# Queries, keys and values laid out queue by queue in a retention and mixture-of-experts kernel

## The chip, the cores and the metric

The kernel runs on one core of one Trainium2 chip. The metric is the device time of one execution in microseconds (us). Before the change it is 428.4 us, the median of three runs (426.91, 428.40, 432.99).

## The reference

A retention layer (attention with a decay in the place of the softmax) over 8 batches, 8 heads, 576 positions and 64 values per head, then a layer of 8 experts on the 4608 tokens of width 512 that come out. The core of it:

```python
scores = scale * np.matmul(q, k.transpose(0, 1, 3, 2))
Dmat = np.where(rel >= 0, gamma[:, None, None] ** rel[None, :, :], 0.0)
attn = np.matmul(scores * Dmat[None, :, :, :], v)

x = attn.transpose(0, 2, 1, 3).reshape(B * S, H * D)
do_compute = x @ w_skip > 0          # other tokens stay as they are
xc = x[do_compute]
e_idx = np.argmax(xc @ w_gate, axis=1)
for e in range(E):
    mask = e_idx == e
    y[mask] = gate_w[mask, None] * (np.maximum(xc[mask] @ w1[e], 0.0) @ w2[e])
out[do_compute] = xc + y
```

## The kernel before

The retention runs chunk by chunk. A group g (36 of them, `NT`) is 128 tokens: one chunk of 64 positions of two batches, all 8 heads. Nine groups in a row (`NQ`) make up the sequence of one pair of batches. Each group has a tile `u` of 128 partitions and 4 x 512 values of 4 bytes, so 8 KB per partition and 1 MB in all: the first half (s = 0 and 1) holds queries and keys for the scores, the second half (s = 2 and 3) holds values and keys by rows for the running state. Five such tiles exist (`UBUFS`).

The loop over g does one step per group. TensorE (PE) interleaves the state product of g (L528) with the scores of g + 1 (L476), then multiplies the values of g - 1 (L556), transposes the finished group g - 2 (L578), and now and then works on the router's logits (L586) and on ranks (L233). VectorE (DVE) multiplies the scores by the decay and puts them back into `u` (L494), and takes the products out (L567). GpSimd (POOL) scales the keys of g + 2 by a decay into `kn` (L514), which reads the second half of that group's `u`; two `kn` buffers exist. ScalarE (ACT) copies the state into the next group's `u` (L539), takes the transposed rows out (L580) and issues their store to `out` (L581).

All loads of `u` are issued on SyncE (SP), one for each half, at L436 in `load_half`: 72 of them, 512 KB each. Four groups are loaded ahead of the loop (`UAHEAD`). In step g, the second half of group g + 3 is issued behind the first block of products (a dependency written by hand on the last product so far), and the first half of group g + 4 behind the products of the values of g - 1, which free the buffer. So a half is issued some two and a half to three and a half steps before TensorE needs it. The order on TensorE is the program's own (a manual schedule); other engines keep the order that the tile framework gives them.

In the array that the host prepares, `qkv`, the 512 KB of one load lie in one piece: 128 rows, one per partition, of 1024 values (4096 bytes), group after group and half after half.

From 137.5 us on SP also loads the first expert's weights (L130, 512 KB each, register-addressed), with 64 such loads over the whole program. The experts follow, one after another: two matrix products (L387) with weights and activations each split into a high and a low part (L139, L140), gathers of tokens from `out` (L303) and scatters of results to it (L836).

Of the kernel before, what the change touches and what calls it, by code (L numbers as in the profile page):

```python
# [22 lines left out]
NTOK, DM, NE, DF = B * S, H * D, 8, 1024  # L23
P = 128
NT = NTOK // P
# [2 lines left out]
NCC = DM // P  # L28
NFC = DF // P
NBLK = 3  # L30

CAPS = (368, 344, 332, 308, 304, 286, 278, 276)
CAP = CAPS[0]
# [23 lines left out]
def kernel(  # L57
# [36 lines left out]
    make_identity(nc, ident)  # L94
    iota = const.tile([P, NBLK * P], F16, tag="iota", name="iota")
    nc.gpsimd.iota(iota, pattern=[[1, NBLK * P]], base=0, channel_multiplier=0, allow_small_or_imprecise_dtypes=True)
    desc = const.tile([P, NE], F32, tag="desc", name="desc")
# [79 lines left out]
    def route_b(ps, first, late, pin, n, t0, ex, mb, cb):  # L177
        c0 = NE * NCMP * NBLK + t0 * NE
        pr = ps[:, c0 : c0 + n * NE]
# [44 lines left out]

    def slot_match(t, nb=NBLK):

        r = rs_t[t] = rt.tile([P, NBLK * P], BF16, tag="r", name=f"r_{t}", bufs=NR)
        nc.vector.tensor_scalar(r[:, : nb * P], iota[:, : nb * P], trank[:, t : t + 1], None, ALU.is_equal)  # L228

    def slot_add(ps, t, first, last, nb=NBLK):  # L230
        r = rs_t.pop(t)
        for k in range(nb):
            nc.tensor.matmul(  # L233
                ps[:, k * NE * NCMP : (k + 1) * NE * NCMP],
                r[:, k * P : (k + 1) * P],
                mc[:, t, :],
                start=first and k == 0,
                stop=last,
                skip_group_check=True,
            )  # L240
# [174 lines left out]
    with ExitStack() as actx:  # L415
# [17 lines left out]
        def load_half(g, s, after=None):  # L433
            if s == 0:
                u_t[g] = ap.tile([P, 4, 2, NPR, D], F32, tag="u", name=f"u_{g}", bufs=UBUFS)
            half = nc.sync.dma_start(  # L436
                u_t[g][:, s : s + 2].rearrange("p s c a i -> p (s c a i)"),
                qkv[g, s // 2],
            )
            if after is not None:  # L440
                tc.add_manual_dep(
                    half.ins,
                    after.name,
                    mybir.DependencyInfo(mybir.DependencyClass.Sync, mybir.DependencyReason.DATA),
                    reason="the second half begins behind a block of products",
                )

        def load_u(g):
            for s in (0, 2):
                load_half(g, s)  # L450
# [241 lines left out]
        for g in range(NT):  # L692
            ahead = g + 1 < NT
            for c in range(2):
                in_turn(state(g, c), *([scores(g + 1, c)] if ahead else []))
                if c == 0 and g and g + UAHEAD - 1 < NT:
                    load_half(g + UAHEAD - 1, 2, last_product())
# [8 lines left out]
            if g + UAHEAD < NT:  # L706
                load_half(g + UAHEAD, 0)
# [15 lines left out]
        g = NT  # L723
# [332 lines left out]
```

## Time and profile before

| | |
|---|---|
| median of three runs | 428.4 us |
| the profiled execution | 428.38 us |
| its span, first to last instruction | 426.6 us |
| mean granted TensorE clock | 0.971 |
| HBM read, written | 77.98 MB, 14.55 MB |
| loads of `u` from `qkv` | 72, of 512 KB each |
| first and last issue of them | 0.8 and 146.5 us |
| loads of weights | 64, of 512 KB each |
| stores of `out` by the retention | 36, of 256 KB each |

The profile's engines are PE (TensorE's matmul; PEld its weight load, which runs beside it), DVE, ACT, POOL and SP; a name with a q behind it (SPq, PEq) is the engine's sequencer, where DMAs are issued and waits are held. A name like L436 is a line of the kernel. A row such as "psc<-u" names the tile written and the tile read. The busy strips cut the span into 40 slices of 10.7 us with the busy share in tenths. "DMA share" is the mean busy share of the core's 16 DMA engines. The queue q1 carries what SP issues, q10 what ACT issues, q0 what POOL issues; q8 and q14 bring instructions. Landing is the time from a DMA's issue to its completion.

### The profile page before, as it was taken

The numbers are of one execution on the slowest core, as the hardware profiler recorded it, in microseconds if no ns is written. First come the engines' busy times: TensorE is split into PE (matmuls) and PEld (weight loads), VectorE is DVE, ScalarE is ACT, GpSimd is POOL, SyncE is SP. The second block draws the span as 40 slices with busy tenths as digits, with TensorE's granted clock in tenths as the row PEclk, the third lists the DMA queues.
The fourth block names the chain that finished last, engine by engine and source line by source line (L and its number), as shares of the span: only waits on it lengthen the run. The fifth ranks groups of instructions, "written<-read, shape, count | busy, mean of one in ns | idle before, by whom it ended". The sixth has DMA issues, their size and how long they took to land.

```text
span 426.6 us, 13158 instructions
## 1 busy us (share of the span) xinstructions
PE 383.3 (90%) x5482; PEld 349.2 (82%) x5484; DVE 272.9 (64%) x570; ACT 176.1 (41%) x296; POOL 148.9 (35%) x166
## 2 busy tenths in 40 slices
PE   7888777978796878999999999999999999999990
PEld 3676666866675756888999999999999999999980
DVE  2567694688579888948745565775665665656430
ACT  1334343354344446216444434444534445455210
POOL 5833643364365468060150043032042151400302
PEclk9989998999999889999999999999999999999996
DMA  8889997999989985363765456456456466652101
GB/s 305 310 290 339 311 325 249 328 334 305 311 296 349 338 315 163 103 220 117 267 201 181 148 171 211 149 189 205 163 177 221 154 222 204 199 157 89 52 2 53
DMA packets 29135, 93.05 MB, mean 218 GB/s; under 512 B 3960, under 2 KB 4344, under 8 KB 29072
## 3 DMA queue, kind: packets, MB, share of 16 engines
q1 hardware_dynamic: 19584, 71.31, 50.2%
q0 software_dynamic: 3728, 11.04, 7.6%
q10 hardware_dynamic: 5760, 9.82, 6.1%
q8 instruction: 44, 0.72, 0.7%
q14 instruction: 19, 0.16, 0.1%
HBM read 77.98 MB, written 14.55 MB: 217 GB/s over the span
## 4 chain that ended last, share of the span: by engine, by line
PE 44%; DMA 22%; issue 16%; DVE 10%; POOL 4%; ACT 1%; another core or an unknown queue 1%; POOLq 0%; ACTq 0%; SPq 0%
DMA out<-rs,sidx 15%; PE py L387 10%; PE ph L387 9%; PE pxt L556 7%; PE ps_s L528 5%; PE px L578 4%; DMA xg<-out,gidx 3%; PE psc L476 3%; DVE u L494 2%; POOL out L836 2%; DVE r L228 2%; PE pl L586 2%; DMA out<-xn 1%; DMA u<-qkv 1%; POOL xg L303 1%
## 5 line engine op out<-in xcount | busy, mean ns | idle before, releaser
L140 DVE TENSOR_TENSOR wlo_w<-w,whi_w 128x1024 fp32r<-128x1024 f32 x59 | 71.9, 1223 | 56.5 <-ACT whi_w L139 56.4
L514 POOL TENSOR_TENSOR kn<-u,tt_sb 64x512 f32<-64x512 f32 x64 | 67.5, 1054 | 74.3 <-DMA u<-qkv 51.5
L836 POOL DMA_INDIRECT out<-rs,sidx x24 | 32.7, 1363 | 151.0 <-DVE rs L835 147.7
L139 ACT CAST whi_w<-w 128x1024 fp32r<-128x1024 f32 x59 | 61.6, 1051 | 57.5 <-PE py L387 53.9
L387 PE MATMUL py<-hhi,whi_w 128*128 128x344 f32 (+6 forms) x224 | 70.2, 313 | 0.0
L494 DVE TENSOR_TENSOR u<-psc,dt_sb 64x512 f32<-64x512 f32 x72 | 49.6, 689 | 30.9 <-PE psc L476 15.7
L387 PE MATMUL ph<-xhi,whi_w 128*128 128x344 f32 (+6 forms) x224 | 68.9, 307 | 0.0
L387 PE MATMUL py<-hhi,wlo_w 128*128 128x344 f32 (+6 forms) x224 | 67.7, 302 | 0.0
L387 PE MATMUL ph<-xhi,wlo_w 128*128 128x344 f32 (+6 forms) x224 | 67.7, 302 | 0.0
L387 PE MATMUL ph<-xlo,whi_w 128*128 128x344 f32 (+6 forms) x224 | 67.7, 302 | 0.0
L387 PE MATMUL py<-hlo,whi_w 128*128 128x344 f32 (+6 forms) x224 | 67.5, 302 | 0.0
L539 ACT COPY u<-ps_s 64x512 f32<-64x512 f32 x64 | 37.1, 579 | 46.7 <-PE psc L476 18.3
L528 PEld LDWEIGHTS ps_s<-u,kn 64*64 64x64 f32 x1024 | 36.9, 142 | 21.5 <-issue 13.1
L476 PE MATMUL psc<-u 64*64 64x64 f32 x1152 | 47.8, 230 | 7.0 <-issue 6.9
L556 PE MATMUL pxt<-u 128*64 128x64 f32 x1152 | 46.0, 233 | 8.3 <-issue 8.3
L395 ACT ACTIVATE hhi<-ph 128x344 fp32r<-128x344 f32 (+8 forms) x61 | 26.0, 426 | 64.3 <-PE ph L387 62.1
L528 PE MATMUL ps_s<-u,kn 64*64 64x64 f32 x1024 | 43.2, 231 | 9.9 <-issue 8.4
L556 PEld LDWEIGHTS pxt<-u 128*64 128x64 f32 x1152 | 39.9, 145 | 13.6 <-issue 11.3
L476 PEld LDWEIGHTS psc<-u 64*64 64x64 f32 x1152 | 41.0, 141 | 8.1 <-issue 7.7
L387 PEld LDWEIGHTS ph<-xhi,whi_w 128*128 128x128 f32 x224 | 42.3, 189 | 0.1
L387 PEld LDWEIGHTS ph<-xlo,whi_w 128*128 128x128 f32 x224 | 42.3, 189 | 0.1
L387 PEld LDWEIGHTS py<-hlo,whi_w 128*128 128x128 f32 x224 | 42.3, 189 | 0.0
(178 smaller groups left out, 641.3 us busy)
## 6 DMA issues: line engine op xcount, KB each, us to landing
u<-qkv SPq DMA_DIRECT2D x72, 512.0 KB, 5.8
w<-w SPq DMA_DIRECT2D x64, 512.0 KB, 3.6
out<-xn ACTq DMA_DIRECT2D x36, 256.0 KB, 5.9
out<-rs,sidx POOLq DMA_INDIRECT x24
xg<-out,gidx POOLq DMA_INDIRECT x21
dt_sb<-dtab ACTq DMA_DIRECT2D x1, 128.0 KB
gt_sb<-dtab ACTq DMA_DIRECT2D x1, 128.0 KB
wg_sb<-wg ACTq DMA_DIRECT2D x1, 64.0 KB, 8.3
```

Source lines behind the costliest of these rows:

```text
L139: nc.scalar.copy(hi, t)
L140: nc.vector.tensor_tensor(lo, t, hi.bitcast(F32), ALU.subtract)
L387: nc.tensor.matmul(ps, x, y, start=first and n == 0, stop=last and n == 3 * len(terms) - 1)
L395: nc.scalar.activation(hi, ph, AF.Relu)
L476: nc.tensor.matmul(psc_t[g][halves[j], c, a, :], u[halves[j], 1 - j, c, a, :], u[halves[j], j, c, a, :], start=c == 0 and a == 0, stop=c = ...
L494: nc.vector.tensor_tensor(u_t[g][h, j], psc[halves[j]], tab, ALU.mult)
L514: nc.gpsimd.tensor_tensor(kn_t[g][h], u_t[g][h, 2 + j], tab, ALU.mult)
L528: nc.tensor.matmul(ps_s[halves[j], c, a, :], kn_t[g][h, c, a, :], u_t[g][h, 3 - j, c, a, :], start=n == 0 and c == 0 and a == 0, stop=c == ...
L539: nc.scalar.copy(u_t[g + 1][halves[j], 3 - j], ps_s[halves[j]])
L556: nc.tensor.matmul(pxt[halves[j], a, c * D : (c + 1) * D], u_t[g][:, 3 - j, c, a, :], u_t[g][:, j, c, a, :], start=c == 0 and a == 0, stop ...
L578: nc.tensor.transpose(px[:, c * P : (c + 1) * P], xt_t[b][:, c, o * P : (o + 1) * P], ident)
L836: put = nc.gpsimd.indirect_dma_start(out=out, out_offset=bass.IndirectOffsetOnAxis(ap=sidx[:n, k, e : e + 1], axis=0), in_=rs[:n], in_offs ...
```

## The change

The host puts `qkv` into another order. Its 128 rows per load are seen as 16 times 8, and the 16 becomes the outermost dimension of the whole array: first all of piece 0 (8 rows of group 0's first half, 8 rows of its second half, 8 rows of group 1's first half, and so on), then all of piece 1. A piece has 36 x 2 x 8 rows of 4096 bytes, which is 2.36 MB. The load takes the same 128 rows into the same 128 partitions: its source is now 16 runs of 32 KB at a distance of 2.36 MB instead of one run of 512 KB. In the access pattern of the DMA that is a dimension of 16, one of 8 and one of 1024 values on the side of the source, against 128 partitions and 1024 values on the side of the tile; before, both sides had 128 and 1024.

No instruction is added, removed or moved on any of the engines, and no wait is changed.

```diff
+NQUEUE = 16
...
 def load_half(g, s, after=None):
     if s == 0:
         u_t[g] = ap.tile([P, 4, 2, NPR, D], F32, tag="u", name=f"u_{g}", bufs=UBUFS)
     half = nc.sync.dma_start(
         u_t[g][:, s : s + 2].rearrange("p s c a i -> p (s c a i)"),
-        qkv[g, s // 2],
+        qkv[:, g, s // 2],
     )
...
+    def by_queue(x):
+
+        x = x.reshape(*x.shape[:2], NQUEUE, P // NQUEUE, x.shape[-1])
+        return np.ascontiguousarray(x.transpose(2, 0, 1, 3, 4))
+
...
-    qkv = qkv.reshape(NT, 2, P, 2 * DM)
+    qkv = by_queue(qkv.reshape(NT, 2, P, 2 * DM))
```

## The prediction

> **What bounds the kernel now.** I read the page first (span, busy shares, the strip of 40 slices), then the busy times by stretches, the waits, the instructions on tile u, the DMA view cut to the stretch in which qkv is loaded, and the chain at the start.
>
> The page:
>
> ```profile
> span 426.6 us, 13158 instructions
> ...
> PE   7888777978796878999999999999999999999990
> ...
> DMA  8889997999989985363765456456456466652101
> ```
>
> Some 15 of 40 slices (160 us) have DMA engines at 8 or 9 tenths and PE at 7 or 8; then PE is full and DMA half used. The qkv loads lie in the first part, so the change can act there alone. The stretches give that in numbers (columns: stretch, length, busy time of PE, PEld, DVE, ACT, POOL, granted clock, mean DMA share, GB/s):
>
> ```profile
> 20.00:146.00 126.00, 102.46 (x3003) 84.94 (x3005) 92.87 (x214) 52.69 (x93) 57.11 (x58) 0.97 0.91 311
> 165.00:426.00 261.00, 248.46 (x1810) 240.81 (x1806) 156.10 (x312) 109.19 (x181) 64.07 (x55) 0.99 0.50 161
> ```
> ```profile
> 40.00:60.00 20.00, 15.01 (x437) 12.22 (x435) 15.45 (x36) 7.69 (x14) 11.66 (x12) 1.00 0.96 318
> 60.00:80.00 20.00, 17.02 (x505) 14.84 (x500) 12.82 (x27) 8.72 (x15) 6.22 (x6) 0.91 0.81 270
> ```
>
> From 20 to 146 us PE is busy 102.46 of 126 us (81%) while the 16 DMA engines are at 0.91; the fullest 20 us slice has 0.96. Neither stands far ahead of the other. The waits in 10 to 160 us (who waited for whom: us in total, times, longest):
>
> ```profile
> POOL kn L514 <- DMA u<-qkv: 47.6, 22, 8.3
> ...
> PEld ps_s L528 <- issue: 13.1, 20, 2.7
> ...
> PEld pxt L556 <- issue: 10.4, 8, 2.2
> ...
> PEld psc L476 <- issue: 7.2, 6, 2.3
> ...
> PEld ps_s L528 <- POOL kn L514: 5.7, 9, 0.8
> ```
>
> POOL, which scales the keys, waits 47.6 us for qkv. Almost none of it reaches PE: its weight loads wait 5.7 us for kn, and 30.7 us (13.1 + 10.4 + 7.2) for nothing that the profile names. So PE's own stream sets the pace today and the loads run just ahead of it. The step, from tile u (duration min/median/max in ns, first and last start in us):
>
> ```profile
> L476 PE MATMUL psc<-u x1152: 212/218/366, 6.2 to 159.5; 64*64 64x64 f32 x192
> ...
> L436 SPq DMA_DIRECT2D u<-qkv x72: 327/328/1040, 0.8 to 146.5; - x72
> ...
> DMA to landing us min/median/max: 4.1/5.8/7.7
> ```
>
> The scores of 36 groups run from 6.2 to 159.5 us: 35 steps of 4.38 us. What a step asks of the DMA engines is in the DMA view cut to 10 to 146 us (packets, MB, share of 16 engines; then issues):
>
> ```profile
> q1 hardware_dynamic: 9484, 34.53, 75.2%
> q10 hardware_dynamic: 4102, 7.48, 14.5%
> ...
> u<-qkv SPq DMA_DIRECT2D x62, 512.0 KB, 5.7
> out<-xn ACTq DMA_DIRECT2D x30, 256.0 KB, 5.9
> w<-w SPq DMA_DIRECT2D x3, 512.0 KB, 7.9
> ```
>
> Loads: 75.2% of 136 us is 102.3 us of each engine for 34.53 MB, 65.9 transfers of 0.524 MB: 1.55 us of every engine for one, 21.1 GB/s per engine. Stores: 14.5% is 19.7 us for 7.48 MB, 23.7 GB/s, 0.66 us for one. A step has two loads and one store: 2 x 1.55 + 0.66 = 3.76 us of 4.38. The rest of the 0.91 are instruction packets and, late, weights.
>
> **The change part by part.** No engine gets an instruction more or in another place; the program's order is the same on all five. Three things change.
>
> *The issue on SP.* Its source access now has three dimensions (16 pieces, 8 rows, 1024 values) where it had two. What this costs SP no row shows; the bounds are the usual 328 ns and the longest issue, 1040 ns. SP has room:
>
> ```profile
> SPq L436 <- PE pxt L556: 57.3, 30, 4.9
> SPq L436 <- PE psc L476: 44.7, 31, 4.1
> ```
>
> It spends 102 us of the first 147 waiting for PE (a free buffer, and the dependency put in by hand). 72 issues longer by 0 to 0.7 us put landings up to 0.7 us later, against a lead of some two and a half steps, 11 us, of which 5.8 go to the landing. I take 0; if the cover were gone, it would be 0.7 x 36 = 25 us at most, which the range holds.
>
> *The place in memory.* One row stays 4096 bytes; eight rows that follow one another for a queue lay in one run before, if a queue had eight neighbouring rows, and still do. [...] Bounds: at best a load runs at the stores' rate, 1.55 x 21.1/23.7 = 1.38 us; at worst reads fall on the same place and it slows to any degree. I take no change, since a run of 32 KB is 8 packets long and its beginning is a small part.
>
> *Which rows a queue moves.* This is where I expect the time to come from. Both sides of the old transfer counted 128 rows, and how they were dealt out to 16 queues isn't in the trace. [...] Bounds from the rows: a load costs 1.38 us where nothing stops it (the stores' rate) and twice that, 2.76 us, if two queues always meet. [...]
>
> [...]
>
> Sum: 72 loads x (2.07 - 1.55) = 37 us more on each DMA engine. Slack takes (0.96 - 0.91) x 146 us = 7 us. The rest, 30 us, lands on the path: 2 x 2.07 + 0.66 = 4.80 us and the 0.2 us of other packets exceed 4.38 x 0.96 = 4.20 us, the 5 us of lead are eaten in some eight steps, and from then on PE waits for kn and for u. A part of PE's 30.7 us without a named cause will fall into those waits; I take 1 us off for it. The first products move too:
>
> ```profile
> 0.82 0.40 SPq L436
> ...
> 1.27 5.48 DMA u<-qkv
> ...
> 6.92 1.05 POOL kn L514
> ```
>
> The 5.48 us contain two loads, so about 1 us more; it is in the 72. From 165 us on nothing changes (weights keep their form), so the delay is carried to the end unaltered. The profiled execution took 428.38 us with a span of 426.6, and the median of the three is 428.4, so both bases agree: 428.4 + 29 = 457 us.
>
> **The rivals.**
>
> *Nothing happens* (0.23). Rows of 4096 bytes, eight for a queue, 16 queues, as before. For it: nothing in the trace says that two queues meet, and PE, not DMA, set the pace at 0.91. [...] Time: 428, with the issues up to 431.
>
> *Faster* (0.07). One long run per queue takes away the gap between 21.1 and 23.7 GB/s: 72 x 0.17 = 12 us of DMA time, and each POOL wait gets shorter. Of that PE can gain the 5.7 us it waits for kn, and some of its unnamed 30.7 us if instruction packets get through sooner. It decides if loads come under 1.45 us: 428 - 8 = 420 us. Against it: PE stays busy 81% and waits mainly for something else.
>
> *Reads meet in memory* (0.06). Sixteen streams at one distance of 2.36 MB may fall on the same part of it. At a load of 2 us the price is as above; at twice today's 1.55 us it is 72 x 1.55 - 7 = 105 us, 533. It counts as slower. [...]
>
> *Always met* is the far end of the forecast: 72 x (2.76 - 1.55) - 7 = 80 us, 508 us. The near end, factor 1.25 (1.73 us), is 72 x 0.17 - 7 = 5 us, 434.
>
> **How the numbers follow.** Queues that meet: 0.64, with 457 as the likeliest and 439 to 488 (factors 1.3 to 1.8) as its own range. Nothing: 0.23. Faster: 0.07. Memory: 0.06. A measurement of this kernel tells about 2%, 8.6 us, from no change. Slower takes 0.64 + 0.06 less the near end below 437, 0.02: 0.68. Same takes 0.23 + 0.02, 0.25. Faster 0.07. The range of 426 to 490 leaves out the faster case, a little of the second, and the far ends of both slow ones, together some 0.2.
>
> **What would show it.** Right: the loads' share in 10 to 146 us above 80% at fewer GB/s than 311; the landing of u above 7 us; POOL's wait for u grown well beyond 47.6 us and PE or PEld waiting for kn, or DVE for u, by 20 us or more; the steps at about 5.2 us; stores still at 23.7 GB/s, which would speak for SBUF's write side and against HBM as a whole; from the last step on a trace that is only shifted. Wrong: the loads' time per transfer still at 1.55 us (then nothing met), or below 1.45 (then the place in memory paid). A longer issue shows as more than 328 ns on SP with landings that aren't longer.

## The result, and the profile after

The changed kernel takes 453.64 us (median of four runs, 451.76 to 460.73) against 430.69 us (four runs, 426.91 to 436.17): ratio 1.055, 95% interval 1.042 to 1.068. It is slower, by 23 us. The ratio leaves out one run of each kernel that lies over 1.5% above the fastest of its kernel.

The page of the changed kernel: its span, and the strips of PE and of the DMA engines (40 slices of 11.25 us).

```profile
span 450.0 us, 13158 instructions
...
PE   6868787778769676999999999999999999999990
...
DMA  8999999998999999526377445645646566563101
```

As many instructions as before, and the DMA strip has moved up to 9 nearly everywhere in the first 16 slices. The same stretch as before by busy time (columns as in the prediction: PE, PEld, DVE, ACT, POOL, clock, DMA share, GB/s), then the whole stage up to the last scores, first of the kernel before and then of the changed one:

```profile
20.00:146.00 126.00, 98.56 (x2778) 81.57 (x2779) 82.93 (x177) 48.08 (x85) 53.67 (x54) 0.93 0.98 281
```
```profile
0.00:159.50 159.50, 129.76 (x3586) 104.21 (x3588) 113.37 (x251) 64.85 (x111) 80.11 (x106) 0.95 0.90 315
```
```profile
0.00:182.70 182.70, 138.32 (x3586) 109.58 (x3588) 116.44 (x251) 64.83 (x111) 82.40 (x108) 0.88 0.97 276
```

The DMA engines went from 0.91 to 0.98 while they moved less per second: 281 GB/s for 311. The stage takes 182.7 us for 159.5, with the same 3586 matmuls. Of these 23.2 us, 14.6 are PE idle (44.4 for 29.7) and 8.6 are PE busy for longer on the same work: the granted clock fell from 0.95 to 0.88. Behind the stage the trace is only shifted: 450.0 - 182.7 = 267.3 us, before 426.6 - 159.5 = 267.1.

What a load costs, in the DMA view cut to 10 to 146 us, and tile u:

```profile
q1 hardware_dynamic: 8535, 31.06, 82.9%
q10 hardware_dynamic: 3668, 6.58, 14.5%
```
```profile
L477 PE MATMUL psc<-u x1152: 212/218/367, 6.5 to 182.7; 64*64 64x64 f32 x192
...
L437 SPq DMA_DIRECT2D u<-qkv x72: 536/537/1672, 0.8 to 163.6; - x72
...
DMA to landing us min/median/max: 4.5/7.1/13.8
```

82.9% of 136 us is 112.7 us of each engine for 59.2 loads: 1.90 us each, before 1.55. A store takes 19.7 us / 25.1 = 0.79 us; before it was 19.7 us / 28.5 = 0.69. Issues got longer, from 328 to 537 ns, and the landing rose from 5.8 to 7.1 us.

At the start, eight loads stand in the queues and nothing else is of any size (from 5 to 15 us q1 has a share of 93.7% in both kernels, q10 8.5% before and 11.4% after). Busy times from 5 to 15 us, before and after:

```profile
5.00:15.00 10.00, 7.78 (x169) 5.30 (x169) 4.07 (x6) 1.16 (x2) 7.18 (x9) 0.83 1.03 400
```
```profile
5.00:15.00 10.00, 6.57 (x104) 4.15 (x103) 4.94 (x6) 0.00 (x0) 3.88 (x5) 0.76 1.05 257
```

Both have the DMA engines full (shares of 1.03 and 1.05), and the rate is 400 GB/s in the one and 257 in the other. This row is the price of the change without anything around it: a factor of 1.56. In the packet records of the trace the same: a row of 4096 bytes takes 159 ns there before (median of 905 in these 10 us), and 262 ns after.

### The profile page after: what moved, and what is told of

It is laid out like the page before. It is cut to its first block, busy times and chain, and to the rows that moved or that the text cites. A ratio compares the mean times of both kernels' runs of the same rounds, so it can differ in the third digit from the quotient of the medians.

```text
span 450.0 us, 13158 instructions
## 1 busy us (share of the span) xinstructions
PE 392.7 (87%) x5482; PEld 356.0 (79%) x5484; DVE 275.5 (61%) x570; ACT 176.4 (39%) x296; POOL 147.1 (33%) x166
## 4 chain that ended last, share of the span: by engine, by line
PE 64%; DMA 17%; issue 10%; DVE 5%; POOL 1%; SPq 0%; ACT 0%; POOLq 0%; DVEq 0%; ACTq 0%
PE py L388 17%; PE ph L388 16%; DMA out<-rs,sidx 11%; PE pxt L557 8%; PE ps_s L529 6%; DMA u<-qkv 5%; PE px L579 4%; PE psc L477 3%; PE pl L587 3%; PE pt L800 2%; DVE r L229 2%; PE yn L834 1%; DMA xg<-out,gidx 1%; PE ph_early L388 1%; DVE u L495 1%
## 5 line engine op out<-in xcount | busy, mean ns | idle before, releaser
L388 PE MATMUL py<-hhi,whi_w 128*128 128x344 f32 (+6 forms) x224 | 70.2, 313 | 0.0
L388 PE MATMUL ph<-xhi,whi_w 128*128 128x344 f32 (+6 forms) x224 | 68.9, 307 | 0.0
L388 PE MATMUL py<-hhi,wlo_w 128*128 128x344 f32 (+6 forms) x224 | 67.7, 302 | 0.0
L388 PE MATMUL ph<-xhi,wlo_w 128*128 128x344 f32 (+6 forms) x224 | 67.7, 302 | 0.0
L388 PE MATMUL ph<-xlo,whi_w 128*128 128x344 f32 (+6 forms) x224 | 67.7, 302 | 0.0
L388 PE MATMUL py<-hlo,whi_w 128*128 128x344 f32 (+6 forms) x224 | 67.6, 302 | 0.0
L477 PE MATMUL psc<-u 64*64 64x64 f32 x1152 | 50.3, 238 | 17.0 <-issue 16.0
L529 PEld LDWEIGHTS ps_s<-u,kn 64*64 64x64 f32 x1024 | 39.1, 150 | 28.5 <-issue 21.9
L529 PE MATMUL ps_s<-u,kn 64*64 64x64 f32 x1024 | 45.4, 239 | 10.6 <-issue 7.1
L477 PEld LDWEIGHTS psc<-u 64*64 64x64 f32 x1152 | 43.5, 149 | 14.1 <-issue 12.1
L557 PE MATMUL pxt<-u 128*64 128x64 f32 x1152 | 48.2, 243 | 5.7 <-issue 5.7
L557 PEld LDWEIGHTS pxt<-u 128*64 128x64 f32 x1152 | 42.4, 154 | 11.7 <-issue 8.6
L388 PEld LDWEIGHTS ph<-xhi,whi_w 128*128 128x128 f32 x224 | 42.3, 189 | 0.1
L388 PEld LDWEIGHTS ph<-xlo,whi_w 128*128 128x128 f32 x224 | 42.2, 189 | 0.1
L388 PEld LDWEIGHTS py<-hlo,whi_w 128*128 128x128 f32 x224 | 42.3, 189 | 0.0
```

The source lines that it names most:

```text
L388: nc.tensor.matmul(ps, x, y, start=first and n == 0, stop=last and n == 3 * len(terms) - 1)
L477: nc.tensor.matmul(psc_t[g][halves[j], c, a, :], u[halves[j], 1 - j, c, a, :], u[halves[j], j, c, a, :], start=c == 0 and a == 0, stop=c = ...
L529: nc.tensor.matmul(ps_s[halves[j], c, a, :], kn_t[g][h, c, a, :], u_t[g][h, 3 - j, c, a, :], start=n == 0 and c == 0 and a == 0, stop=c == ...
L557: nc.tensor.matmul(pxt[halves[j], a, c * D : (c + 1) * D], u_t[g][:, 3 - j, c, a, :], u_t[g][:, j, c, a, :], start=c == 0 and a == 0, stop ...
```

## The experiments

### Place, pieces and issue, one at a time

Three things had changed with one line: where the rows lie, how the access counts them, and how SP issues the load. The first three kernels separate them. Each ratio is to runs of the kernel before that were made beside that experiment.

Rows apart: the 128 rows of a load 295 KB from one another, so eight of them cover 2.36 MB as in the change, with 128 rows on both sides of the access.

```diff
-                qkv[g, s // 2],
+                qkv[:, g, s // 2],
...
-    qkv = qkv.reshape(NT, 2, P, 2 * DM)
+    qkv = np.ascontiguousarray(qkv.reshape(NT, 2, P, 2 * DM).transpose(2, 0, 1, 3))
```

> Each partition's 72 rows lie in one piece of 295 KB, so the 128 rows of a load are 295 KB apart (eight of them 2.36 MB, as in the change), but both sides of the access count 128 rows as before. If the way rows are dealt to the queues costs the time: like before, ratio 0.99 to 1.01, 328 ns per issue, q1 near 1.55 us of each DMA engine per load. If the place in memory costs it: as slow as the changed kernel or slower, ratio 1.05 or more. If the issue costs it: like before.

Measured: 429.11 us, ratio 1.006 (1.001 to 1.012). Busy times from 5 to 15 us, and the loads' row from 10 to 146 us:

```profile
5.00:15.00 10.00, 6.88 (x169) 4.40 (x169) 3.53 (x6) 1.16 (x2) 7.14 (x9) 1.00 1.03 403
```
```profile
q1 hardware_dynamic: 9128, 33.22, 72.4%
```

403 GB/s, and 98.5 us for 63.4 loads, 1.55 us each. Where the rows lie, together or 295 KB apart, makes no difference to the loads.

Pieces near: the 16 pieces of a load lie together as before, with one unused row behind each so that the access can't be counted as 128 rows.

```diff
-                qkv[g, s // 2],
+                qkv[g, s // 2][:, : P // NQUEUE],
...
-    qkv = qkv.reshape(NT, 2, P, 2 * DM)
+    qkv = qkv.reshape(NT, 2, NQUEUE, P // NQUEUE, 2 * DM)
+    qkv = np.concatenate([qkv, np.zeros_like(qkv[:, :, :, :1])], axis=3)
```

> A load's rows lie together again as before, in 16 pieces of 8 rows with one unused row of 4 KB behind each piece, so that the access still counts 16 and 8 on the source's side. If the dealing of rows costs the time: as slow as the changed kernel, ratio 1.04 to 1.07, DMA share 0.98 and about 280 GB/s in 20 to 146 us. If the place in memory costs it: like before, ratio 0.99 to 1.01. If the issue costs it: as slow as the changed kernel, with 537 ns per issue, but with q1 near 1.55 us per load.

Measured: 451.86 us, ratio 1.055 (1.046 to 1.065), the whole loss of the change, with the memory near as before.

```profile
5.00:15.00 10.00, 6.29 (x103) 4.13 (x103) 4.78 (x6) 0.00 (x0) 3.31 (x4) 0.78 1.05 247
```

Long issue: the kernel before, with its layout and its two-dimensional access, but its loads of qkv issued in the general form, which is the switch in the diff and takes SP longer (472 ns an issue for 328).

```diff
+            nc.dge_precook = False
             half = nc.sync.dma_start(
...
+            nc.dge_precook = True
```

> [...] If dealing or place costs the time: 537 ns per issue in place of 328, ratio 0.995 to 1.01. If the issue costs it: 537 ns and ratio 1.04 to 1.07.

Measured: 430.54 us, ratio 1.007 (1.002 to 1.013). The issue took 472 ns and not the 537 expected; where the other 65 ns of the change come from is open. 72 issues longer by 144 ns cost nothing that counts.

```profile
L437 SPq DMA_DIRECT2D u<-qkv x72: 471/472/1192, 0.8 to 145.0; - x72
```

So neither place nor issue: the loss comes with the access that counts 16 pieces of 8 rows, wherever they lie (ratio 1.055 with pieces near and with pieces 2.36 MB apart). (The 144 issues of the halves of columns below take 592 ns each in the median and cost as little.)

### Half the partitions, and its control

That the pieces change which rows a queue moves is the author's guess; the trace doesn't show which queue moves a row. If queues meet where they write into SBUF, and half of the partitions leave them half of the places, a plain two-dimensional load over half of the partitions should be slow as well.

```diff
+            for lo in (0, D):
                 half = nc.sync.dma_start(
-                    u_t[g][:, s : s + 2].rearrange("p s c a i -> p (s c a i)"),
-                    qkv[g, s // 2],
+                    u_t[g][lo : lo + D, s : s + 2].rearrange("p s c a i -> p (s c a i)"),
+                    qkv[g, s // 2, lo : lo + D],
                 )
```

> The layout before; each load is cut into two of 64 partitions (0 to 63, 64 to 127), two-dimensional, in rows of 4096 bytes, 144 issues in place of 72. If two queues meet where they write into SBUF, and 64 partitions reach half of the places at which 16 queues can write: slow without any pieces on the source's side, ratio 1.03 to 1.10, q1 at 1.8 us or more per 512 KB. If the pieces on the source's side slow the reading itself: like before but for 144 issues of about 0.54 us, ratio 0.995 to 1.02, q1 near 1.55 us per 512 KB.

Measured: 466.05 us, ratio 1.092 (1.083 to 1.101). The control cuts each load by columns, so that each part covers all 128 partitions, and issues them in the general form:

```diff
+            nc.dge_precook = False
+            for part in (s, s + 1):
                 half = nc.sync.dma_start(
-                    u_t[g][:, s : s + 2].rearrange("p s c a i -> p (s c a i)"),
-                    qkv[g, s // 2],
+                    u_t[g][:, part].rearrange("p c a i -> p (c a i)"),
+                    qkv[g, s // 2, :, (part - s) * DM : (part - s + 1) * DM],
                 )
...
+            nc.dge_precook = True
```

> Control for the 64-partition loads: again 144 loads of 256 KB in the general form, but each over all 128 partitions and half of the columns (rows of 2048 bytes). If the number and size of the loads made the 64-partition kernel slow: ratio 1.06 to 1.10 here too, and about 230 GB/s in 5 to 15 us. If it was that 64 partitions reach half of the places: ratio 0.995 to 1.03 and 370 to 400 GB/s in 5 to 15 us.

Measured: 432.37 us, ratio 1.006 (1.002 to 1.010). The start of both, halves of the partitions first:

```profile
5.00:15.00 10.00, 5.91 (x102) 3.83 (x102) 3.78 (x6) 0.58 (x1) 5.67 (x7) 0.75 1.06 231
```
```profile
5.00:15.00 10.00, 7.44 (x145) 4.93 (x148) 4.37 (x6) 1.16 (x2) 6.74 (x9) 0.83 0.96 320
```

With 64 partitions 231 GB/s, the slowest of all, with no pieces on the source's side; with 128 partitions and as many loads 320. The 320 miss the expected 370 to 400, at a share of 0.96; which of the rows of 2048 bytes, the 144 issues and their general form that comes from is open, and the time doesn't show it (ratio 1.006). Number and size of the loads are not the cause here; which partitions a load covers is.

### Half of the loads, and other loads

Half of the change: first halves from 16 pieces (the expectation's new dealing; how their rows are dealt to queues isn't in the trace), second halves (`vk`) as before.

```diff
-                qkv[:, g, s // 2],
+                qkv[:, g] if s == 0 else vk[g],
...
+    qkv = qkv.reshape(NT, 2, P, 2 * DM)
+    vk = np.ascontiguousarray(qkv[:, 1])
+    qkv = by_queue(qkv[:, :1])[:, :, 0]
```

> Half of the change: the 36 first halves (queries and keys) come from 16 pieces, the 36 second halves are loaded as before. If a load in the new dealing takes 1.90 us of each DMA engine in place of 1.55 and about 10 us of slack swallow the first of it: 36 x 0.35 - 10 = 3 us, ratio 1.00 to 1.02. If each load costs its share of the whole (the slack does not matter): half of the 5.5%, ratio 1.025 to 1.03. If the two dealings disturb one another, so that nearly all loads run slowly: 1.04 or more.

Measured: 446.24 us, ratio 1.041 (1.033 to 1.049): the third case. The loads' row from 10 to 146 us:

```profile
q1 hardware_dynamic: 8595, 31.29, 81.4%
```

110.7 us for 59.7 loads, 1.85 us on average, when half of them are loaded as before. If the two kinds didn't touch one another, the average would be 1.73. So they do, which is what queues that meet at a common place would do. The packet records point to the old loads as those that pay: from 5 to 15 us, 209 of 660 rows of 4096 bytes take 140 to 170 ns, where half of the loads are old ones; before it was 881 of 905, and in the changed kernel none.

The weights instead of qkv: the 64 loads of the experts from 16 pieces.

```diff
-        nc.sync.dma_start(t.rearrange("p m c i -> p (m c i)"), w[bass.ds(regs[e], 1), f].rearrange("o p c -> (o p) c"))
+        nc.sync.dma_start(t.rearrange("p m c i -> p (m c i)"), w[:, bass.ds(regs[e], 1), f].rearrange("q o r c -> q (o r) c"))
...
+    w = np.ascontiguousarray(w.reshape(NE, NFC, NQUEUE, P // NQUEUE, 2 * DM).transpose(2, 0, 1, 3, 4))
```

> The loads of qkv as before, but the 64 loads of the experts' weights come from 16 pieces of 8 rows each. If the new dealing costs only where the DMA engines are full: landing of a weight load longer than 3.6 us (4 us or more), ratio 0.995 to 1.01, since they are at 0.50 from 165 us on. If every such load delays the end by what it takes longer: 64 x 0.35 = 22 us, ratio 1.04 to 1.06.

Measured: 439.08 us, ratio 1.024 (1.015 to 1.034), between the two expectations. A stretch of this kernel and its loads of weights, then the same of the kernel before:

```profile
300.00:340.00 40.00, 40.00 (x294) 39.95 (x294) 23.50 (x33) 18.54 (x31) 11.39 (x9) 1.00 0.78 197
L131 SPq DMA_DIRECT2D w<-w x64: 539/540/684, 142.6 to 394.7; - x64
...
DMA to landing us min/median/max: 5.1/5.6/12.0
```
```profile
300.00:340.00 40.00, 40.00 (x297) 39.95 (x297) 24.46 (x36) 19.14 (x31) 8.52 (x7) 1.00 0.57 180
L130 SPq DMA_DIRECT2D w<-w x64: 332/333/541, 137.6 to 385.8; - x64
...
DMA to landing us min/median/max: 3.4/3.6/7.9
```

In the experts' stage the slower loads land later, as expected, and only raise the DMA share from 0.57 to 0.78; PE works 40.00 of 40 us in both, and from the second expert's first up-product (L387 before, L388 here) to the last expert's it takes 203.1 us against 202.8. So there the slower loads cost nothing.

Where the 8 us of this kernel come from is open. Between the two profiled executions 9.0 us have to be found (spans of 435.6 and 426.6). The first weights are issued at 142.6 us and not at 137.6, so 5.0 us are there before any changed load is issued, where both kernels do the same work; the granted clock from 20 to 146 us was 0.92 for 0.97. The last scores come at 166.1 us for 159.5, which adds 1.6 us, and the rest lies behind them and ahead of the second expert. So in these two executions at most 4 us can lie with the weights, 1.6 of them where the first weights meet the last loads of qkv.

### How the full DMA engines reach PE

The forecast had PE wait for u and kn. The waits of the changed kernel's PEld, from 10 us to the last scores, don't say that (in total, times, longest):

```profile
PEld ps_s L529 <- issue: 21.9, 25, 2.7
PEld psc L477 <- issue: 12.1, 8, 3.6
PEld pxt L557 <- issue: 8.1, 5, 2.9
...
PEld ps_s L529 <- POOL kn L515: 4.1, 4, 2.3
...
PEld psc L477 <- DMA u<-qkv: 1.1, 1, 1.1
```

PEld's waits for kn and u are about as small as before (4.1 us for kn now, 5.7 before); what grew are waits for nothing that the profile names: PEld's three on ps_s, psc and pxt from 30.7 to 42.1 us. In the packet records these pauses stand in a pattern. Queue q8 brings instructions in packets of 16 KB, 28 up to the last scores. Before the change PE has 21 pauses over 0.2 us there after the first 10 us, 26.3 us in all, and 19 of them (25.7 us) end within 1.9 us behind the end of a q8 packet, 1.4 us in the median. After the change 22 of 27 do, with 36.6 of 40.7 us. With the packets' times shifted at random it would be 9.5 and 12.1 us on average. Up to the last scores PE has 3586 products and 3588 weight loads in both kernels, 256 of them for each of the 28 packets; whose instructions a packet holds isn't in the trace.

Three kernels take the loads' consumers away. From group 4 on the loads run at the same places of the program into tiles that nothing reads, and the groups compute on the first four groups' tiles; in the last one there are no such loads.

```diff
+            if g < UAHEAD:
                 if s == 0:
-                    u_t[g] = ap.tile([P, 4, 2, NPR, D], F32, tag="u", name=f"u_{g}", bufs=UBUFS)
+                    u_t[g] = ap.tile([P, 4, 2, NPR, D], F32, tag="u", name=f"u_{g}", bufs=UAHEAD)
+                to = u_t[g][:, s : s + 2]
+            else:
+                if s == 0:
+                    u_t[g] = u_t[g - UAHEAD]
+                to = ap.tile([P, 2, 2, NPR, D], F32, tag="aside", name=f"aside_{g}_{s}", bufs=NASIDE)
...
-                load_half(g + UAHEAD, 0)
+                load_half(g + UAHEAD, 0, last_product())
```

> The changed kernel, but from group 4 on the loads of qkv (same places in the program, same 16 pieces, at most four in flight) go to tiles that nothing reads, and the groups compute on the first four groups' tiles again; the routing then is another one, so only the time up to the last scores counts (182.7 us in the changed kernel). If PE is late because loads land late: the last scores come at 155 to 162 us as in the kernel without pieces, with fewer unnamed waits. If PE is late because its instructions come late while the DMA engines are full: 168 us or later, and PE's unnamed waits stay at 40 us or more.

> The same with the layout and the 128-row access of before; also here from group 4 on the loads go to tiles that nothing reads and the first groups' tiles are computed on again. If loads that land late are what makes the change slow: last scores within 3 us of the kernel with pieces and no reader. If instructions that come late: 8 us or more earlier than that one, at 150 to 160 us.

> No loads of qkv from group 4 on at all (the first groups' tiles are computed on again, the routing is another one). If PE's unnamed waits come from instructions that are late while the DMA engines are full: they fall below 15 us up to the last scores, which come at 145 us or earlier. If they have nothing to do with the DMA engines: they stay at 25 us or more, last scores at 152 to 160 us.

One run each; other tokens then go to other experts, so only the time up to the last scores can be compared. Busy times up to there: pieces without a reader, rows without a reader, no loads.

```profile
0.00:186.20 186.20, 136.81 (x3588) 108.62 (x3588) 115.78 (x251) 63.99 (x111) 81.61 (x107) 0.88 0.97 267
```
```profile
0.00:159.20 159.20, 128.05 (x3588) 102.14 (x3588) 116.51 (x251) 64.56 (x111) 79.39 (x106) 0.95 0.89 314
```
```profile
0.00:141.10 141.10, 123.26 (x3588) 99.53 (x3588) 115.42 (x251) 64.75 (x111) 79.56 (x106) 0.96 0.33 118
```

With nothing waiting for the loads from group 4 on, the last scores come at 186.2 us with pieces and at 159.2 with rows, as in the two real kernels (182.7 and 159.5). Of these 27 us some 8 are there by the scores of group 5, which begin at 32.0 and 24.2 us: the first four groups' loads still have readers. The other 19 come after them, where it isn't the loads' landing that holds PE. PE's pauses behind q8 packets are 39.1 us of 43.7 with pieces and 21.6 of 27.6 with rows. With no loads they fall to 6.0 of 15.0, which is what packets shifted at random would give (6.0), and the stage to 141.1 us, 4 us under its bound. The unnamed waits of PEld without loads, from 10 us to the last scores:

```profile
PEld px L582 <- issue: 7.7, 8, 2.5
PEld ps_s L532 <- issue: 7.6, 18, 1.7
...
PEld pxt L560 <- issue: 1.5, 2, 0.8
PEld psc L480 <- issue: 1.3, 2, 0.8
```

On ps_s, pxt and psc they fall from 30.7 to 10.4 us (without a reader they are 43.2 us with pieces and 32.0 with rows). With those on px, whose products wait by name for VectorE, and 0.7 on the router's logits it is 18.8 us, over the 15 that the expectation set. What the three kernels show is that the DMA engines' fullness reaches PE without any data dependency on the loads; that the instruction packets carry it is the reading that fits best, by the time at which the pauses end, but no kernel changed the instruction packets alone.

Where loads really do hold PE, it looks different. PEld's waits with the loads of 64 partitions, from 10 us to the last scores at 196 us:

```profile
PEld ps_s L529 <- ACT u L540: 38.0, 28, 3.9
PEld psc L477 <- DMA u<-qkv: 12.0, 12, 2.5
...
PEld ps_s L529 <- issue: 3.3, 3, 2.3
```

There PE waits by name for the state (whose copy in turn waits 61.2 us for kn) and for u, the unnamed waits on ps_s, pxt and psc are down to 8.8 us from 30.7, and of 47.9 us of pauses only 22.0 end within 1.9 us behind a q8 packet.

## Why the prediction was right

The forecast was 457 us with a range of 426 to 490, by queues that meet; measured are 453.64. The cost of the loads was foreseen; the way on which it reaches the end was not, so that the sum comes this near is in part luck. Its steps:

*What bounds the kernel.* The prediction said that PE's own stream sets the pace and that the DMA engines at 0.91 stand just behind. Right, and more than was meant: with no loads the stage is 18 us shorter (141.1 for 159.5) and PEld's unnamed waits on its three products are a third, so these were tied to the DMA engines, too.

*The issue on SP, taken as 0.* Right: 537 ns for 328, and issues alone lengthened to 472 ns gave ratio 1.007.

*The place in memory, taken as no change.* Right: rows apart took 1.55 us a load, as the kernel before. The rival of reads that meet in memory is out, and so is the faster one.

*Which rows a queue moves.* Right as far as it goes: pieces near show that the access that counts 16 pieces costs the time (ratio 1.055), and half the partitions (1.092), its control (1.006) and half of the loads (1.041) fit the writing side. That two queues meet at one place in SBUF is the author's guess at the cause and the best reading of these five kernels; neither the queues' rows nor the place were seen. What was seen is the time of a row: from 5 to 15 us, with the DMA engines full, 4096 bytes take 159 ns in the median before, 262 in the changed kernel and 295 with the loads of 64 partitions.

*The size of the load's term.* The forecast took 2.07 us, 1.5 times the 1.38 us that a load would take at the stores' rate. No run shows the 2.07 us or the factor of 1.5, which was the author's estimate; the changed kernel's loads took 1.90 us, 1.23 times the 1.55 of before. That is 72 x 0.35 = 25 us of DMA time and not 37. The other way, stores were taken to stay as they are and went from 0.69 us to 0.79, 36 x 0.10 = 4 us; and the engines filled to 0.98 and not 0.96, so the slack took some 10 us and not 7. By the prediction's own sum that is 25 + 4 - 10 = 19 us; the stage grew by 23. Two figures of the working are off without weight: its 0.66 us for a store is 0.69 by its own row (19.7 us for 28.5 stores of 0.262 MB), and a lead of 5 us is used up in six steps and not eight, at 4.80 + 0.2 - 4.20 = 0.8 us a step.

*How it reaches the end.* This step failed. It said that the lead of the loads is used up and that "from then on PE waits for kn and for u", by 20 us or more, and that a part of the unnamed waits would fall into these. PEld's waits for kn and u hardly moved, and the unnamed ones grew. The kernels without a reader show most of the same loss with no dependency on the loads. What stands in its place: 14.6 us more of PE idle, of which the pauses behind instruction packets are 10.9 (36.6 for 25.7), and 8.6 us of PE busy for longer at a clock of 0.88 for 0.95, which the forecast didn't have; why the clock fell is open. Both are more than the differences between executions: rows apart and long issue have 32.3 and 29.1 us idle at 0.94 and 0.93, pieces near 44.8 at 0.87. Only the start is as foretold: the value products begin at 19.9 us for 15.2, because POOL has to wait for the first loads (8.7 us up to 22 us, before 4.9 us up to 17). That this way costs PE about as much as the forecast had put on late data is luck; no step of the prediction gives it.

*The signs named.* Share above 80%, fewer GB/s, landing above 7 us, POOL's wait for u (71.7 us from 10 us to the last scores) and the pure shift came as said. The step of (182.7 - 6.5) / 35 = 5.03 us is a little under the 5.2. Stores did not keep their rate: 20.9 GB/s per engine for 23.7. So the one sign that was to tell SBUF's write side from the rest is missing, and the write side rests on the experiments alone.

## What to carry to other kernels

The shape of a load's access can cost more than where its rows lie: here 128 rows as the outermost count on both sides were best, and memory could be rearranged inside that (rows 295 KB apart had 403 GB/s), while a source counted as 16 pieces fell from 400 GB/s to 257, and a load over 64 partitions to 231. Look for the price in a stretch in which only such loads run. Whether it matters was here a question of how full the DMA engines were: in the retention, at a share of 0.98, the slower loads cost 23 us; the experts' weight loads, from the second expert on and at a share of 0.78, landed 2.0 us later and cost nothing. And when PE pauses for nothing that the profile names, set its pauses beside the instruction packets before looking for a data dependency.

## What was not expected of the hardware

- PE's pauses go with the instruction packets of q8 where the DMA engines are nearly full (a share of 0.90 up to the last scores): 25.7 us of them in the kernel before end within 1.9 us behind a packet of 16 KB, and 6.0 us, no more than chance, with the loads taken away (a share of 0.33).
- Two loads of 64 partitions are slower than 16 pieces over 128: 231 and 257 GB/s, where one load of 128 partitions has 400.
- Loads from 16 pieces and loads as before disturb one another: 1.85 us on average for a mixture of equal parts, against 1.55 and 1.90 for the pure ones, whose mean is 1.73.
- Stores, which read SBUF, went from 0.69 to 0.79 us beside the slower loads.
- Issues of one load of 512 KB on SP took 328, 472 or 537 ns by the form of the access; 472 ns by itself did not show in the time (ratio 1.007).
